# One explicit order of small steps for a chunked recurrence and its MLP on one core

## The chip, the core and the metric

The kernel runs on one core of one Trainium2 chip. The core has five engines that run at the same time and meet through semaphores: TensorE (PE in the profile; its weight loads are PEld), VectorE (DVE), ScalarE (ACT), GpSimd (POOL) and SyncE (SP, which here only issues transfers). Sixteen DMA engines move data between the device memory and the core's SBUF. TensorE writes into PSUM, which the kernel cuts into four tiles of 2 x 512 float32 per partition.

The metric is the time of one execution in microseconds (us) on the device, as a median of runs; less is better.

## The reference

The first half is a recurrence over 768 tokens for 4 batches x 8 heads, with a 40 x 40 state per head:

```python
for t in range(S):
    y[:, :, t] = np.einsum('bhd,bhde->bhe', rt, state)
    Sa = np.einsum('bhde,bhe->bhd', state, at)
    state = state * wt[:, :, None, :] - np.einsum('bhd,bhe->bhde', Sa, bt) \
            + np.einsum('bhd,bhe->bhde', vt, kt)
```

Its output, 3072 rows of 320, goes through an MLP with an exact GELU and 2048 hidden columns:

```python
h = x @ w_in                                    # 320 x 2048
g = 0.5 * h * (1.0 + erf(h / sqrt(2)))
out = g @ w_out                                 # 2048 x 320
```

All inputs of the recurrence are float32. The two weights come out of the set-up as float64, 5.24 MB each; the kernel reads them as pairs of 32-bit words and makes float32 of them on the core.

## The kernel before

**Chunks.** The tokens are cut into 12 chunks of 64 (`C = 64`, `NCH = 12`). In one chunk all 32 heads of all batches are worked on together. The products inside a chunk replace the loop over tokens: the logarithms of w are summed along the chunk (`logs`, `sums`), a, b and k are scaled by the running decays (`scale_a`, `scale_b`, `scale_k`), and four masked 64 x 64 products per head are made: N (b with a), A (k with a), RV (r with v) and M. Since the rank-one term uses the state that it changes, each chunk needs the inverse of a unit triangular 64 x 64 matrix made of N, per head.

**The inverse.** Each 64 x 64 matrix is taken as two triangular 32 x 32 blocks and a corner. `make_N` (L598) makes N in SBUF and stores its diagonal blocks to a scratch tensor in device memory (L615). `start_inverse` (L651) loads them back as `Nb` so that one partition holds one block (L664), and GpSimd builds the inverse `W` column by column: 31 pairs of a product (L672) and a sum (L674). `store_inverse` (L680) writes `W` out again, and `fetch_inverse` (L689) brings it back in the layout of the products, as `Tt` and `T2`. `turn_corner` (L771) transposes it on VectorE into `L`, and `corner` and `joined` (L775, L790) put the corner in with two sets of small matmuls, both into tiles named J. From chunk 2 on the inverse of chunk c+2 is started while chunk c is worked on. The first chunk goes another way: `squares` (L712) inverts its blocks by repeated squaring on TensorE, five stages of 128 small matmuls.

**The chain of a chunk.** With the inverse and the state of the chunk before: `make_X`, `make_sa`, `make_saT`, `make_M`, `make_y2`, `make_QY`, and then `outputs` (L880), which writes the chunk's MLP input `xt`, moves parts of it between partitions by eleven small transfers, and updates the state.

**The MLP.** `mlp(c)` (L986) is a generator: four pieces of the first product, of 40 matmuls each into one PSUM tile, with one GELU each, then the second product. For the first three chunks this is the plain product; from the fourth on `seven` (L937) does it as seven block products instead of eight, with sums of weight blocks made once (`weight_sums`, L929) and sums of activations made by VectorE in each chunk. These pieces fill TensorE's time between the steps of a chunk: `fill()` (L1025) takes the next piece.

**The weights.** `first_load` and `second_load` bring in the words; `to_float` (L312) converts a piece. With VectorE as its engine it is five VectorE operations and one on ScalarE; with GpSimd, three on VectorE, three on ScalarE and two additions on GpSimd (seven of the ten w_in pieces).

**The order.** Each engine works through its own instructions in the order in which the program issues them, and the program issues them by hand: a straight list of calls for the first two chunks (L1060 on) and a loop over the rest (L1247). SP issues almost all transfers, and a transfer that must wait holds up those behind it. Three kinds of calls only keep TensorE busy: `warm` (L1054), `keep` (L92), which makes the next `duo` (L96) begin with such matmuls, and an opening burst of three products.

## Time and profile before

| | |
|---|---|
| time, median of 3 runs | 717.69 us (715.69 to 719.35) |
| span of the profiled execution | 717.1 us (the page gives no other time for it) |
| TensorE busy | 680.9 us (95%) |
| VectorE busy | 365.9 us (51%) |
| GpSimd busy | 348.0 us (49%) |
| ScalarE busy | 222.2 us (31%) |
| first product of the MLP on TensorE (L994) | 220.0 us busy, 1920 instructions |
| second product, seven blocks (L947) / plain (L1011) | 146.4 us / 56.3 us busy |
| moved by DMA | 74.46 MB, mean 104 GB/s |

A float32 matmul call appears in the trace as two instructions, so 40 calls show as x80 and a half piece of the first product (10 calls) as x20. In rows of the timeline the first number is the start in us from the start of the span, the second the length in us; a line number is that of the call or of a helper (all small matmuls have L110), so that the tile names tell them apart. "[12.77 <-DMA Nb<-N]" says that the engine had been idle for 12.77 us until that transfer landed.

### The profile page before, as it was taken

What the parts mean: (1) busy time and instruction counts of PE and PEld (TensorE: products, weight loads), DVE (VectorE), ACT (ScalarE), POOL (GpSimd) and SP (SyncE); (2) the same over time, 40 slices, a digit from 0 to 9 for tenths busy, and PEclk for the clock granted to TensorE, in tenths of its full rate; (3) what the DMA queues carried; (4) which work ended last, traced back from release to release, by engine and by line L of the source; (5) the groups of instructions that cost most, each with busy time, mean ns of one, the idle gap of its engine ahead of it and who ended that gap; (6) DMA issues with size and microseconds to landing.
All of it is one profiled execution on the core that took longest, in us unless ns stands there. A gap on an engine that the chain in (4) does not pass through costs nothing.

```text
span 717.1 us, 32807 instructions
## 1 busy us (share of the span) xinstructions
PE 680.9 (95%) x14816; PEld 584.5 (82%) x14816; DVE 365.9 (51%) x481; ACT 222.2 (31%) x308; POOL 348.0 (49%) x798
## 2 busy tenths in 40 slices
PE   7898897869999999999999999999999999999997
PEld 5565586757777877899899898998998898998987
DVE  2223689995255266276374583573672772522303
ACT  5123575444141240350351332232223413112020
POOL 4374258820760861861862843835826817800000
PEclk8799999989999999999999999999999999999999
DMA  9599437953665755655747646657748553020100
GB/s 132 102 173 151 97 84 185 157 113 87 129 125 96 127 118 94 133 105 94 146 96 128 132 90 125 125 97 127 144 70 155 115 101 66 21 54 3 28 11 18
DMA packets 287923, 74.46 MB, mean 104 GB/s; under 512 B 265736, under 2 KB 284456, under 8 KB 287784
## 3 DMA queue, kind: packets, MB, share of 16 engines
q1 hardware_dynamic: 283360, 68.20, 51.4%
q0 software_dynamic: 864, 2.36, 2.1%
q8 instruction: 116, 1.90, 1.2%
q10 hardware_dynamic: 3560, 1.80, 1.0%
q14 instruction: 23, 0.19, 0.1%
HBM read 58.69 MB, written 9.70 MB: 95 GB/s over the span
## 4 chain that ended last, share of the span: by engine, by line
PE 77%; DVE 3%; SPq 2%; ACT 2%; issue 1%; DMA 1%; ACTq 1%; DVEq 0%
PE ph L994 29%; PE po L947 19%; PE po L1011 7%; PE QY L110 6%; PE J L110 2%; PE X L110 2%; PE av L110 1%; PE sap L110 1%; PE saT_ps L110 1%; PE A_ps L110 1%; PE RV_ps L110 1%; PE M_ps L110 1%; PE N_ps L110 1%; SPq L898 1%; PE wT_ps L110 1%
## 5 line engine op out<-in xcount | busy, mean ns | idle before, releaser
L994 PE MATMUL ph<-xt,w_in_sb 64*128 64x256 f32 x1920 | 220.0, 381 | 0.4 <-issue 0.4
L994 PEld LDWEIGHTS ph<-xt,w_in_sb 64*128 64x128 f32 x1920 | 183.3, 187 | 22.8 <-issue 1.7
L672 POOL TENSOR_TENSOR tmp<-W,Nb 128x126 f32<-128x126 f32 (+22 forms) x310 | 121.3, 391 | 159.4 <-DMA Nb<-N 136.4
L674 POOL TENSOR_TENSOR W<-W,tmp 128x126 f32<-128x126 f32 (+22 forms) x310 | 133.2, 430 | 24.3
L996 ACT ACTIVATE gt<-ph 128x1024 f32<-128x1024 f32 x48 | 49.1, 1023 | 152.3 <-PE ph L994 152.2
L947 PE MATMUL po<-w_out_sb,gt 128*128 128x160 f32 x576 | 82.9, 302 | 1.0 <-DVE gt L967 1.0
L947 PEld LDWEIGHTS po<-w_out_sb,gt 128*128 128x128 f32 x576 | 78.7, 190 | 3.1 <-DVE gt L967 1.3
L1011 PE MATMUL po<-w_out_sb,gt 128*128 128x320 f32 x192 | 56.3, 451 | 2.2 <-ACT wpT L443 2.2
L1011 PEld LDWEIGHTS po<-w_out_sb,gt 128*128 128x128 f32 x192 | 37.0, 197 | 18.1 <-ACT wpT L443 2.5
L803 DVE COPY Tt<-J 32x512 f32<-32x512 f32 x9 | 6.2, 689 | 55.8 <-ACT Tt L803 55.8
L787 ACT COPY Js<-J 128x256 f32<-128x256 f32 x11 | 4.1, 370 | 94.2 <-PE J L110 94.2
L186 DVE STREAM_TRANSPOSE aT<-a_pairs 128x1024 f32<-128x1024 f32 x9 | 11.2, 1246 | 42.3 <-DMA a_pairs<-in_a_dram 42.3
L999 DVE TENSOR_TENSOR half<-gt 128x1024 f32<-128x1024 f32 x9 | 11.4, 1269 | 30.5 <-ACT gt L996 30.4
L951 DVE TENSOR_TENSOR os<-os,po 128x160 f32<-128x160 f32 x36 | 11.5, 319 | 28.9 <-PE po L947 23.2
L947 PE MATMUL po<-extra,half 128*128 128x160 f32 x176 | 26.1, 303 | 0.0
L575 DVE TENSOR_TENSOR SM<-M_ps,upper 128x1024 f32<-128x1024 f32 x12 | 14.5, 1207 | 22.3 <-PE M_ps L110 22.3
L320 ACT ACTIVATE conv<-conv,rebias 128x320 uint32<-128x320 uint32 (+1 forms) x26 | 16.1, 623 | 29.7 <-DVE conv L319 23.3
L947 PEld LDWEIGHTS po<-extra,half 128*128 128x128 f32 x176 | 24.2, 190 | 0.3
L996 ACT ACT_TABLE_LOAD x10 | 12.8, 1283 | 37.1 <-PE ph L994 37.1
L110 PE MATMUL warm<-cum_m,ident 128*128 128x512 f32 x40 | 23.8, 736 | 0.0
L662 POOL MEMSET W<- 128x512 f32 x10 | 5.3, 529 | 35.8 <-DMA inv<-W 35.8
L947 PE MATMUL po<-extra,gt 128*128 128x160 f32 x144 | 21.0, 299 | 0.0
(224 smaller groups left out, 1133.2 us busy)
## 6 DMA issues: line engine op xcount, KB each, us to landing
Nb<-N SPq DMA_DIRECT2D x20, 256.0 KB
VR<-in_v_dram SPq DMA_DIRECT2D x24, 160.0 KB
out_dram<-os SPq DMA_DIRECT2D x48, 80.0 KB
b_rows<-in_b_dram SPq DMA_DIRECT2D x22, 160.0 KB
k_rows<-in_k_dram SPq DMA_DIRECT2D x22, 160.0 KB
N<-N SPq DMA_DIRECT2D x44, 64.0 KB
Tt<-inv SPq DMA_DIRECT2D x44, 64.0 KB
a_pairs<-in_a_dram SPq DMA_DIRECT2D x18, 144.0 KB
```

The costliest lines, as they stand in the source:

```text
L110: nc.tensor.matmul(o, lhsT, rhs, start=first, stop=True, skip_group_check=True)
L186: nc.vector.transpose(to.rearrange("p n (s y) -> p n y s", y=2), raws.pop((c, n)).rearrange("p n (y d) -> p n y d", y=2)[:, :, :, :BL])
L320: nc.scalar.activation(power, power, ACT.Relu, bias=rebias, scale=8.0)
L575: nc.vector.tensor_tensor(to, pt, upper.unsqueeze(1).to_broadcast([P, 2 * G * NP, C]), ALU.mult)
L672: eng.tensor_tensor(t, W[:, :rows, j:j + 1].to_broadcast([P, rows, rest]), Nb[:, j:j + 1, j + 1:].to_broadcast([P, rows, rest]), ALU.mult)
L674: eng.tensor_tensor(W[:, :rows, j + 1:], W[:, :rows, j + 1:], t, ALU.add)
L947: nc.tensor.matmul(po[:, n, :DM // 2], l_[:, f], r_[:, f], start=f == 0, stop=f == NF // 2 - 1)
L951: nc.vector.tensor_tensor(to, one_, other, ALU.add)
L994: nc.tensor.matmul(ph[:, x, s], w_in_sb[half(x), kt, p * P:(p + 1) * P], xt[half(x), kt], start=kt == 0, stop=kt == NK - 1)
L996: nc.scalar.activation(gt[:, 4 * q:4 * q + 4].rearrange("p (x s) t -> p x s t", x=2), ph, ACT.Gelu)
L999: nc.vector.tensor_tensor(s1, block(1, 0), block(1, 1), ALU.add)
L1011: nc.tensor.matmul(po[:, g], gt[:, f, g * P:(g + 1) * P], w_out_sb[:, f], start=f == 0, stop=f == NF - 1)
```

## The change

The hand-written list, the loop and the fill calls go. Every piece of work becomes a generator under a short name, `N`, `inv`, `ph` and so on, whose `yield`s cut it into steps; a string `ORDER` of tokens, one per step, is the order in which all steps of all chunks are issued. A token `ph0:2` is the next step of `ph` for chunk 0, and the number after the colon is the PSUM tile (or conversion buffer) that it takes: four fixed PSUM tiles take the place of a pool that gave them out in turn. Tiles of SBUF are laid out once.

Beside the order itself: no token calls `warm`, and nothing like `keep` is left; the opening burst has six products. The squarings of the first chunk work on two halves of the blocks (`sq0`, `sq1`), with the additions of the identity on VectorE. All weight pieces are converted without GpSimd. A step of the first product is half a piece; one GELU still covers two steps. The second product of the last chunk is the plain one, after a step (`ws4`) that restores a weight block. N of chunk c+1 is made in chunk c, after `corner` of chunk c. Inverses are stored from SP for chunks 1 and 2 and from GpSimd for the others, as before. The decays that scale b and k overwrite the tile of w.

```diff
+POOLED_IN, POOLED_OUT = (), ()
+SCALED_BY_POOL = (0,)
+COPIED_BY_ACT = (1, 2)
+INVERSES_BY_POOL = 3
...
+ORDER = """
+tails0 begin6 w0 begin6:0 consts0 logs0 sums0:1 sums0:2 w1 logs1 sums0 sums0 b0 sums1:3 sc0 sums1:0 a0 zeros4 sums1 b1
+sc1 sums1 gaps0 ta0:2 ta0 pads0 pads3 tb0:1 a1 tails1 ta1:0 gaps1 tb0 N0:3 ta1 r0 tr0:2 tr0 v0 wi0 wi1 k0 N0 sq0 pads1
+tb1:1 sq1 r1 sq1 sq0 sq0:0 sq1:3 zeros0 tb1 sq1 N1:2 sq0 sq0 zeros3 sq1 zeros1 tv0:1 N1 N1 sq1:3 tv0 k1 sq1 sq1 sq1
+sq0:0 r2 sq0 sq0 sq0 RV0:1 ci3:0 b2 ci3 nb1 RV0 pads2 sq0:2 sq0 sq1:3 sq1 sq0 sq0 sq1 inv1 sk0 tk0:0 sq0:1 ci0:1 sq1
...
+ta2 wo0 tn1:0 v2 ci2 tv1 tb2:1 tb2 ci6:1 tk2:2 X1:3 wo2 ci7:2 tk2 tn1 N2:1 N2 N2 ci5:0 ph0:2 ph0 ci6 ci7 ci7 X1 ci5
+ci5 ph0 ph0:0 ph0 wo1 corner1:2 ci8:0 corner1:1 corner1 ci8 A2:3 zeros7 joined1:2 ci6 joined1 joined1 wo4 ph0 A2 RV1:1
...
+co14 co15 co12 co12 ph1 inv2 inv2 ft2 k4 r4 ph1:1 ph1 co13:1 co13 corner2:2 corner2:2 co13 po0 po0 po0 po0 inv3
...
+ph5 ph5 ph5 ph5:1 ph5 ph5 ph5:2 ph5 inv6 inv6 inv6 inv6 tk7:1 ft6 r8 corner6:2 corner6:3 ph5 corner6 v7 RV6:0 RV6
+joined6:1 a8 joined6 joined6 X6:2 inv7 X6 sk7 N7:3 po4 N7 A7:0 A7 saT6:1 saT6 sa6:2 po5:0 sa6 yy6:3:0 M6:1 M6 po5:2
+po5 N7 nb7 tv7 RV7:1 RV7 vp8 QY6 QY6 po5:1 po5 po5 po5:2 po5 po5 w8 y6 logs8 state6 po5 y6 po5 po5:1 po5 tn7:0 po5 ta8
...
+    duos = [psum.tile([P, 2, 512], FP32, tag=f"duo{i}", name=f"duo{i}") for i in range(4)]
...
+    @step
+    def ph(c):
+
+        for q in range(NF // 4):
+            pt = duo().rearrange("p x (s t) -> p x s t", s=2)
+            for s in range(2):
...
+                yield
+            nc.scalar.activation(gt[:, 4 * q:4 * q + 4].rearrange("p (x s) t -> p x s t", x=2), pt, ACT.Gelu)
+            yield
...
+    @step
+    def po(c):
+
+        if c < NS or c == NCH - 1:
+            pt = duo()[:, :, :DM]
+            for piece in range(NF // 4):
+                for g in range(G):
+                    for f in range(4 * piece, 4 * (piece + 1)):
+                        nc.tensor.matmul(pt[:, g], gt[:, f, g * P:(g + 1) * P], w_out_sb[:, f],
+                                         start=f == 0, stop=f == NF - 1)
+                    yield
...
+    for token in ORDER.split():
+        name, *at = token.split(":")
+        places[:] = [int(x) for x in at]
+        if name not in going:
+            kind = name.rstrip("0123456789")
+            going[name] = steps[kind](int(name[len(kind):]))
+        next(going[name], None)
```

The tokens that the text speaks of: `w`, `a`, `b`, `k`, `v`, `r` are loads of a chunk's inputs, `vp`, `bp`, `kp` second loads of v, b and k in another layout; `wi`, `wl`, `wo` are loads of weight words, `ci` and `co` their conversions (w_in in ten pieces, w_out in sixteen); `ta`, `tb`, `tk`, `tv`, `tr`, `tn` are transposes (tn of the state), `sc` and `sk` the scalings of b and k. A chunk's inverse is `N` (product, mask, store), `nb` (the fetch into `Nb`), `inv` (GpSimd's columns and the store), `ft` (the fetch into `Tt` and `T2`), `corner` (`L`, then J) and `joined`. `y` writes `xt` and issues its eleven transfers, `state` updates the state, `ph` is the first and `po` the second product of the MLP.

## The prediction

> **What bounds the kernel now.** I read the page first (shares, slices), then the windows on both sides of one instant, then the timeline around the inverses, then the chain of waits. In the fences "J" is the first product that needs the inverse of a chunk (tile J from L and N), the point where a chunk's chain starts.
>
> ```profile
> span 717.1 us, 32807 instructions
> ...
> PE 680.9 (95%) x14816; PEld 584.5 (82%) x14816; DVE 365.9 (51%) x481; ACT 222.2 (31%) x308; POOL 348.0 (49%) x798
> ...
> PE   7898897869999999999999999999999999999997
> ...
> PEclk8799999989999999999999999999999999999999
> ```
>
> TensorE is 95% busy; holes lie in the first nine slices (18 us each). The windows split the span where the third chunk's J starts (157.1). The first two rows are of all instructions; their first pair is the length and PE's busy time. The third is the same stretch for the tile `warm` alone.
>
> ```profile
> 0.00:157.00 157.00, 130.04 (x3144) 97.40 (x3144) 94.28 (x142) 72.57 (x98) 87.91 (x190) 0.92 0.72 132
> 157.00:717.00 560.00, 550.82 (x11672) 487.12 (x11672) 271.59 (x339) 149.58 (x210) 260.11 (x608) 0.99 0.51 96
> ...
> 0.00:157.00 157.00, 29.32 (x46) 10.08 (x46) 0.92 0.72 132
> ```
>
> After 157 PE idles 9.2 us of 560: nothing but less work can shorten that part. Before 157 it is busy 130.0, of which 29.3 is `warm` and 3.7 more the same filler under other tiles (1.1, 1.0, 0.6, 0.5, 0.5 in the groups by form): about 97 us of needed work in 157. So the gain, if any, is PE work brought forward into the first 157 us.
>
> What sets 157.1 is the inverse of chunk 2, a relay over SP, POOL, SP, DVE:
>
> ```profile
> 116.88 0.24 POOL L672 TENSOR_TENSOR tmp<-W,Nb 128x31 f32<-128x31 f32 x1
> ...
> 148.49 0.23 POOL L674 TENSOR_TENSOR W<-W,tmp 128x16 f32<-128x16 f32 x1
> 149.43 1.28 SPq L686 DMA_DIRECT2D inv<-W  x2
> 153.71 1.93 SPq L696 DMA_DIRECT2D Tt<-inv  x4
> ...
> 156.22 0.71 DVE L773 STREAM_TRANSPOSE L<-Tt 128x512 f32<-128x512 f32 x1
> 157.08 0.89 PE L110 MATMUL J<-L,N 32*32 32x32 f32 x64 [3.37 <-DVE L L773]
> ```
>
> The same relay for a later chunk, to be kept for the change:
>
> ```profile
> 528.70 1.11 PE L110 MATMUL N_ps<-aT,nT 40*64 40x64 f32 x64
> ...
> 532.59 2.02 SPq L615 DMA_DIRECT2D N<-N  x4
> 536.23 1.14 SPq L664 DMA_DIRECT2D Nb<-N  x2
> 542.19 0.24 POOL L672 TENSOR_TENSOR tmp<-W,Nb 128x31 f32<-128x31 f32 x1 [12.77 <-DMA Nb<-N]
> ...
> 574.52 1.64 POOL L686 DMA_DIRECT2D inv<-W  x2 [0.30 <-POOL W L674]
> 579.12 0.85 SPq L696 DMA_DIRECT2D Tt<-inv  x2
> ...
> 582.84 0.71 DVE L773 STREAM_TRANSPOSE L<-Tt 128x512 f32<-128x512 f32 x1 [0.75 <-DMA Tt<-inv]
> ```
>
> N's product to L takes 54.1 us here. PE does not wait, because N is made two chunks ahead.
>
> **The change, part by part.** The sum is made against the profiled execution, span 717.1, 0.6 under the median 717.69; its page gives no other time.
>
> *Work.* The matmuls stay, but for three things. All filler goes (33.0 us); the opening burst grows from 3 to 6 products (six instructions took 0.85 us each, later ones of that shape 0.43: about 7.7 us from 1.6 to 9.3, so chunk 0's first product starts near 9.3 and not 7.4; covered by the wait for transfers below). The last second product takes eight blocks: 4.50 + 4.50 + 8.81 = 17.8 us by chunk 3's rows against 15.4 for the seven at the end: +2.0 to 2.4; I take **+2.0**. Restoring the weight quarter is one 1.5 us DVE operation beside the last first product. Half pieces of the first product issue the same 40 matmuls and one GELU per 1024 columns: nothing.
>
> *Conversions.* Seven of the ten w_in pieces lose two POOL additions (1.4 us each) and gain two DVE operations (0.69): 9.7 us more DVE. Beside POOL's additions the DVE steps were stretched (L321 0.42 to 1.04 us, L319 0.42 to 0.75, L324 0.69 to 0.96 on four pieces: 4.9 us), which goes: net +5. The new order gives DVE about 57 us of work between J of chunk 1 and J of chunk 2, against some 70 us of time: hidden, at nothing. If that cover is gone, each further us of DVE there is a us. The Trainium skill, SBUF — State Buffer, Who interferes with whom, says that a DVE instruction with two SBUF inputs waits out a GpSimd one that reads SBUF, and the reverse. By that rule the out-weight steps beside the inverse stay stretched (3.0 us a piece at 128.4 to 131.3 against 2.4 without), some 10 us more for sixteen; the sum would still be hidden.
>
> *First inverse in halves.* Five squarings ran from 30.7 to 60.4 with filler between; interleaved halves need DVE 15.7 and PE 16.7 us of work, but K of chunk 0 now follows two w_in loads, so I put its end at about 45 and chunk 0's state near 62 (before: 86.9). That is not what is late next: the inverse of chunk 1 is. SP now has, ahead of its fetch of N, eight input loads (327 KB each), wi0 and wi1 (2.1 MB), five more inputs and the store of N. At the windows' 127 to 138 GB/s for inputs (20 us, then 12 us) and 173 GB/s at 0.80 DMA share for w_in (10.5 us), plus 7 for N's way out and in, the fetch lands at 50 (before: 36.9). POOL's 31 columns took 27.5 (36.9 to 64.4) or 28.2 (180.6 to 208.8): 78. Store to fetch 4.6, fetch to L 2.5, L to J 0.9: **J of chunk 1 at 87**, as before (87.6), but with eight attention steps and five pieces of the first product already done.
>
> *Chunk 2's inverse.* SP comes to its fetch only after 15 loads behind chunk 1's fetch (8 w_out pairs at 1.3, inputs at 1.6 to 5.4, N 2.0): 31 us after 83, so 114; landing 4.9, POOL 31.8 (116.9 to 148.7), store 5, fetch and L 3.4: **J of chunk 2 at 159**, 1.9 later than now. PE alone would allow 148: from J to J the order has 60 us of PE work.
>
> *What is done by then.* Counted in the order up to that J: 8 of 8 half pieces of ph for chunk 0 and 8 of 8 for chunk 1, 6 of 8 po pieces, two transposes of chunk 3. Before, by 157: 160 ph matmuls (chunk 0's) and 16 of 64 po matmuls. More: 8 x 2.26 + 4 x 2.2 + 2 x 0.87 = **28.6 us** of PE.
>
> *One chunk of look-ahead less.* N of chunk c+1 is now made just after J of chunk c. PE work between N and its J, by the rows' spacing (ph 2.26, po 2.27, QY 1.5, small products 0.6 to 1.1): 47.8, 49.9, 49.0, 48.2, 48.2, 48.4, 47.2, 48.2, 47.0 us for chunks 3 to 11. The relay in the trace: N to its store 2.65; store to fetch 3.5 to 4.7; fetch to POOL 4.8 to 6.2; POOL 28.2 to 31.4 (less 1.54 for the k scaling, which leaves this place); store to Tt's fetch 4.4 to 6.3; to L 2.5 to 3.7; to J 0.8 and starts 0.3. Median 50.0, fastest 47.1, slowest about 55. PE waits for what is missing: at the medians 15.7 us over nine chunks, at the fastest 0, at the slowest 61. In the new order SP has N's store and fetch side by side in eight of nine chunks, but r, v and a loads stand ahead of N in chunks 6 to 8 and v4, r5 ahead of nb4. I take 49.3 as nearest to the median row: **10 us**.
>
> *End.* The chunk's x rows all go by SP (8.6 us at 468.0, before partly by ACT); 11.3 us of second product cover them. One more us for two copies and four stores: +1.0; waits at 167 (1.1) and 672 (1.0) go.
>
> Sum: 717.1 + 1.9 - 28.6 + 2.0 + 10 + 1.0 - 2.1 = **701.3 us**, forecast 701.
>
> **Rivals.**
> *The relay becomes the bound (slower).* Without waits the sum is 691.3, so 25.8 us of waits undo it: a relay of (433.9 + 25.8) / 9 = 51.1 us on average decides. For it: L waited for Tt in two of the last chunks even with two chunks of room, and 54.1 above. Against it: nothing else stands between the steps in the new order. At 53 us: 43 of waits, **734**. Chance 0.20.
> *No wait at all.* Relay at 47 to 48, J of chunk 2 by PE near 150: 717.1 - 7 - 28.6 + 2.0 - 1.1 = **682**. The fastest rows all have to meet. Chance 0.15.
> *The start is late by DVE.* All 26 conversions at stretched lengths (+16 us) use up the cover; J of chunk 2 at 171: **713**. DVE was at 98% from 100 to 150 before. Chance 0.08.
> *The clock.* Filler gone, PE waits in the first 90 us. Where the trace has no filler and waits of 2 to 3 us (150 to 170), the granted clock fell to 0.87 and 0.79, and 64 sums took 1.99 against 1.16 us at 0.71. If the 57 us before the first J all ran so: 98 us, J at 105, +18: **719**. I give it little, since transfers and POOL, not PE, set that J. Chance 0.07. The Trainium skill, TensorE: Matmul & The Clock Gate, Why this matters for your kernels, asks for no PE gap over about 3 us; by that rule the pads were worth keeping, and the trace agrees so far that the clock fell at such gaps.
>
> **How the numbers follow.** The forecast has 0.50, its own range 690 to 713 (relay 48 to 50.5, J of chunk 2 at 154 to 164). 0.5% of 717.7 is 3.6 us, about what a measurement tells here: faster is under 714, slower over 721. Faster: 0.15 + most of 0.50 + a little of the DVE rival = 0.67; same 0.10 (upper edge of the forecast, DVE and clock rivals); slower 0.23. The range 682 to 724 leaves out half of the no-wait case's low side and most of the relay rival.
>
> **What will show it.** J of chunk 1 near 87 and of chunk 2 near 159, no `warm` but the opening, 16 ph half pieces before 157; from then a chunk every 51 to 52 us with a wait of PE for L of about 1 us in each; last store 5 us after the last matmul. Wrong if J follows J by 54 us or more, or if J of chunk 2 comes after 170.

## The result and the profile after

The kernel after takes 799.11 us (median of 4, 796.02 to 805.32), the kernel before 716.69 us (median of 4, 713.29 to 719.35): a ratio of 1.1145, interval 1.1069 to 1.122. The prediction was 701, with 682 to 724 as its range. It is wrong by its sign, and its line "wrong if J follows J by 54 us or more" came true.

The page of the profile after, its span and busy rows, two rows of slices, the queue that brings the instructions, and the chain that ended last:

```profile
span 795.2 us, 32559 instructions
...
PE 700.3 (88%) x14724; PEld 622.0 (78%) x14724; DVE 368.2 (46%) x504; ACT 212.2 (27%) x295; POOL 339.8 (43%) x781
...
PE   8768998967898997997898998889798899898997
...
PEclk9888989978997997898899798899998899899999
...
q8 instruction: 115, 1.88, 1.0%
...
PE 45%; SPq 17%; POOL 12%; DMA 10%; issue 10%; DVE 3%; ACT 1%; DVEq 0%; ACTq 0%; POOLq 0%
```

TensorE (PE) has 19.4 us more busy time although the 33.0 us of filler are gone, and it idles 94.9 us where it idled 36.2. The holes are no longer in the first slices alone; they come back all along the span, and so does a lowered clock (the mean granted clock is 0.911, before 0.979). The chain that ended last runs over SP's queue, POOL and the transfers for 39% of the span. "issue" (time in which an engine waited for nothing that the profile shows) is 10%, where before it had 1%.

The windows on both sides of J of chunk 2, again in the columns length, PE busy, PE weight loads, DVE, ACT, POOL, granted clock, DMA share, GB/s:

```profile
0.00:168.60 168.60, 140.24 (x3308) 117.55 (x3309) 110.60 (x197) 68.55 (x93) 72.16 (x173) 0.91 0.69 136
168.60:795.20 626.60, 560.06 (x11416) 504.40 (x11416) 257.63 (x308) 143.61 (x202) 267.67 (x608) 0.91 0.43 82
```

These two rows hold the whole account against the sum of 701.3. J of chunk 2 comes at 168.6 and not at 159: +9.6. After it the sum had 550.8 - 28.6 + 2.0 = 524.2 us of PE work and 18.1 of idle time; measured are 560.1 busy, +35.9, and 66.5 idle, +48.4. Together 93.9, which is 795.2 - 701.3. The busy part is put down to the clock, 0.91 where the same kind of work had 0.99; the run with long fill below bears the size out. The idle part is in the waits of PE (us in total, times, longest, over the whole run):

```profile
PE duo L140 <- issue: 51.8, 41, 3.5
PE duo L140 <- DVE conv L826: 19.5, 6, 5.6
```

Of the first, 36.4 us fall after J of chunk 2 (37.5 with 1.1 us of the same kind under another line); of the second, 13.9 us, since its longest wait is the one right at that J:

```profile
168.62 1.08 PE L140 MATMUL duo<-conv,N 32*32 32x32 f32 x64 [5.57 <-DVE conv L826]
```

In the kernel before, the wait for the inverse (L, which in the kernel after is `conv` of L826) and the largest of its issue waits were these:

```profile
PE J L110 <- DVE L L773: 4.1, 2, 3.4
...
PE saT_ps L110 <- issue: 2.1, 2, 1.8
```

**The issue stalls.** The timeline of PE after J of chunk 5; rows of the products between two inverses, with a stall in brackets:

```profile
374.62 1.11 PE L140 MATMUL duo<-Tt,avs 64*64 64x64 f32 x61
...
376.81 0.27 PE L140 MATMUL duo<-Tt,avs 64*64 64x64 f32 x2 [1.08 <-issue]
...
380.28 0.27 PE L140 MATMUL duo<-aT,kT 40*64 40x64 f32 x2 [1.33 <-issue]
...
384.29 0.47 PE L140 MATMUL duo<-rT,late 40*64 40x64 f32 x3 [1.92 <-issue]
384.69 7.40 PE L1030 MATMUL duo<-w_out_sb,gt 128*128 128x160 f32 x32
...
747.94 4.51 PE L1030 MATMUL duo<-w_out_sb,gt 128*128 128x160 f32 x32
```

A stall falls into the middle of one product, where nothing that it reads can be late, and again after 3.5 and 4.0 us. The queue q8 explains the place. Its 115 packets of 16,384 bytes stand against 14,724 matmul and 14,724 weight-load records: 29,448 = 115 x 256 and a rest of 8. Stalls that follow each other begin on the same place of this count, 256 instructions apart (over the whole run the place creeps from the 181st to the 48th, so some entries of the queue must have no record here), 1.2 to 1.8 us after one of those packets ended; a packet takes 1.1 us on average. From a packet's start to the first instruction out of it are 2.2 to 3.0 us. A product of 32 calls is 128 instructions and takes 1.05 us, so 256 of them run out in some 2.2 us and PE waits for the rest of the fetch. One half piece of the first product is 40 instructions in 2.26 us: there the fetch is hidden. Before, long pieces stood between the small products and the 116 fetches cost some 5 us.

The last two rows show what follows a stall: the same 32 matmul records take 7.40 us here and 4.51 later. The windows of the stretch around the third stall, 3.4 us each:

```profile
380.20:383.60 3.40, 2.09 (x128) 1.95 (x128) 1.23 (x1) 0.00 (x0) 0.00 (x0) 1.00 0.48 75
383.60:387.00 3.40, 2.71 (x12) 2.60 (x13) 2.14 (x2) 0.00 (x0) 0.00 (x0) 0.50 0.35 93
387.00:390.40 3.40, 3.40 (x14) 3.40 (x14) 1.34 (x2) 0.00 (x0) 0.68 (x3) 0.50 0.96 185
390.40:393.80 3.40, 3.40 (x92) 3.23 (x95) 0.33 (x1) 1.65 (x3) 2.69 (x10) 1.00 0.88 170
```

A stretch in which PE was busy for 2.09 of 3.40 us is followed by one at half clock, which lasts until a stretch without such holes has gone by. If the clock is always either full or half, as in these rows, then with a mean of 0.911 over 795.2 us, (1 - 0.911) x 2 x 795.2 = 142 us ran at half speed; before, (1 - 0.979) x 2 x 717.1 = 30 us. After J of chunk 2 the clock fell 14 times: eight times behind a stall put down to issue (55 us at half clock), four times behind a wait for L (41 us), twice behind other waits (7 us). The Trainium skill, TensorE: Matmul & The Clock Gate, Why this matters for your kernels, names idle gaps over about 3 us as what brings the clock down; here gaps of 1.1 to 1.9 us did. The Trainium skill, TensorE: Matmul & The Clock Gate, A second HAM failure mode: psum-queue depth-cycling, tells of frequent short idles that do it, and that is the reading which this trace agrees with.

**The relay.** The inverse of chunk 5 in rows of PE, SP, POOL and DVE, from the J before it (306.56) over N (307.32) to its own J (368.28):

```profile
306.56 0.83 PE L140 MATMUL duo<-conv,N 32*32 32x32 f32 x64 [3.26 <-DVE conv L826]
307.32 1.16 PE L140 MATMUL duo<-aT,nT 40*64 40x64 f32 x64
...
312.13 3.09 SPq L658 DMA_DIRECT2D N<-spare  x4
317.15 1.20 SPq L711 DMA_DIRECT2D Nb<-N  x2
...
322.29 0.24 POOL L726 TENSOR_TENSOR tmp<-W,Nb 128x31 f32<-128x31 f32 x1 [18.18 <-DMA Nb<-N]
...
354.31 1.64 POOL L735 DMA_DIRECT2D inv<-W  x2 [0.30 <-POOL W L728]
...
361.76 2.43 SPq L745 DMA_DIRECT2D Tt<-inv  x4
...
367.52 0.70 DVE L826 STREAM_TRANSPOSE conv<-Tt 128x512 f32<-128x512 f32 x1
...
368.28 1.08 PE L140 MATMUL duo<-conv,spare 32*32 32x32 f32 x64 [3.95 <-DVE conv L826]
```

N to J takes 61.0 us here. Means over chunks 3 to 11, read from the same rows of every chunk, beside the terms of the prediction:

| step | in the prediction | before, measured | after, measured |
|---|---|---|---|
| N to its store | 2.65 | 3.0 | 4.9 |
| store to fetch of Nb | 3.5 to 4.7 | 3.9 | 5.3 |
| fetch to POOL's first column | 4.8 to 6.2 | 5.4 | 4.8 |
| POOL | 28.2 to 31.4, less 1.54 | 31.3 | 30.8 |
| POOL's end to the fetch of Tt | 4.4 to 6.3 | 6.3 | 5.9 |
| to L | 2.5 to 3.7 | 4.1 | 3.9 |
| L to J | 0.8 + 0.3 | (waits for PE) | 1.5 |
| N to J | 49.3 taken | 53.5, with 1.1 for the last step and less 1.54 | 57.1 |

From J to the next N are 3.3 us (0.7 to 5.7). J follows J by (723.6 - 239.8) / 8 = 60.5 us. That N to J and J to N add up to this period is so in any order; what shows that the loop binds is that PE stood waiting for L at J of chunks 4, 5, 6, 7 and 9. At the other four J, L lay ready first and PE was late.

The wait for L is 19.5 us of the idle time of the whole run; the stalls are more than twice that.

### The profile page after: what moved, and what is told of

The parts are those of the page before. It is cut to its first block, busy times and chain, and to the rows that moved or that the text cites. A ratio compares the mean times of both kernels' runs of the same rounds, so it can differ in the third digit from the quotient of the medians.

```text
span 795.2 us, 32559 instructions
## 1 busy us (share of the span) xinstructions
PE 700.3 (88%) x14724; PEld 622.0 (78%) x14724; DVE 368.2 (46%) x504; ACT 212.2 (27%) x295; POOL 339.8 (43%) x781
## 4 chain that ended last, share of the span: by engine, by line
PE 45%; SPq 17%; POOL 12%; DMA 10%; issue 10%; DVE 3%; ACT 1%; DVEq 0%; ACTq 0%; POOLq 0%
PE duo L140 19%; PE duo L992 12%; PE duo L1030 8%; POOL W L728 6%; POOL tmp L726 6%; SPq L215 5%; PE duo L1014 4%; SPq L218 2%; SPq L204 2%; PE duo L504 2%; DMA inv<-W 2%; SPq L950 2%; DMA w_tile<-in_w_dram 2%; DMA Nb<-N 2%; DMA r_pairs<-in_k_dram 1%
## 5 line engine op out<-in xcount | busy, mean ns | idle before, releaser
L992 PE MATMUL duo<-xt,w_in_sb 64*128 64x256 f32 x1920 | 213.1, 379 | 1.2 <-DMA xt<-xt 0.8
L992 PEld LDWEIGHTS duo<-xt,w_in_sb 64*128 64x128 f32 x1920 | 188.8, 188 | 24.6 <-issue 4.2
L995 ACT ACTIVATE gt<-duo 128x1024 f32<-128x1024 f32 x48 | 49.2, 1024 | 121.6 <-PE duo L992 121.6
L1030 PE MATMUL duo<-w_out_sb,gt 128*128 128x160 f32 x512 | 80.6, 319 | 1.1 <-issue 1.1
L1030 PEld LDWEIGHTS duo<-w_out_sb,gt 128*128 128x128 f32 x512 | 77.4, 206 | 2.2 <-issue 1.3
L1014 PE MATMUL duo<-w_out_sb,gt 128*128 128x320 f32 x256 | 77.0, 460 | 0.0
L1014 PEld LDWEIGHTS duo<-w_out_sb,gt 128*128 128x128 f32 x256 | 51.0, 203 | 22.7 <-issue 4.6
L140 PE MATMUL duo<-rT,late 40*64 40x64 f32 x1536 | 37.5, 249 | 13.9 <-issue 13.9
L140 PEld LDWEIGHTS duo<-rT,late 40*64 40x64 f32 x1536 | 33.1, 161 | 16.7 <-issue 16.4
L1030 PE MATMUL duo<-extra,conv 128*128 128x160 f32 x256 | 36.8, 302 | 0.0
L1030 PEld LDWEIGHTS duo<-extra,conv 128*128 128x128 f32 x256 | 35.0, 190 | 0.9
L623 DVE TENSOR_TENSOR SM<-duo,upper 128x1024 f32<-128x1024 f32 x12 | 14.6, 1219 | 28.6 <-PE duo L140 28.6
```

Source lines behind the costliest of these rows:

```text
L140: nc.tensor.matmul(o, lhsT, rhs, start=first, stop=True, skip_group_check=True)
L992: nc.tensor.matmul(pt[:, x, s], w_in_sb[half(x), kt, p * P:(p + 1) * P], xt[half(x), kt], start=kt == 0, stop=kt == NK - 1)
L995: nc.scalar.activation(gt[:, 4 * q:4 * q + 4].rearrange("p (x s) t -> p x s t", x=2), pt, ACT.Gelu)
L1014: nc.tensor.matmul(pt[:, g], gt[:, f, g * P:(g + 1) * P], w_out_sb[:, f], start=f == 0, stop=f == NF - 1)
L1030: nc.tensor.matmul(pt[:, n, :DM // 2], l_[:, f], r_[:, f], start=f == 0, stop=f == NF // 2 - 1)
```

## The experiments

Theory A, after these readings: the dense runs of small products are the loss (stalls, then half clock), and the wait for L is what they bring with them. Theory B: the relay's loop is the loss, and PE's stalls fall into time in which it would wait anyway. Theory C: the lowered clock is the loss, and anything that keeps PE busy, long or short, holds it up. Theory D came out of the first runs: both limits lie close together, the loop at 60.5 us a chunk and PE's own pace a little below it, so that either cut alone shows little. In the diffs the places of PSUM after the colon are left out, and the tokens of one chunk stand for all.

**N before J (look).** N, its store and its fetch ahead of the J before, the dense products left together:

```diff
-tb6 tk6 ft5 corner5 corner5 ... joined5 tn5 ta6 N6 RV5 joined5 joined5 saT5 po4 saT5 w7 RV5 N6 N6 sa5 nb6 sa5 A6 A6
+N6 nb6 ft5 corner5 corner5 ... joined5 tn5 RV5 joined5 joined5 saT5 po4 saT5 w7 RV5 sa5 sa5 A6 A6
```

> Edit: from chunk 4 on, the product N, its store and its fetch Nb are moved before the J of the chunk before (N into the first product's pieces), so a chunk's inverse has a chunk more of room; the small products stay back to back. Theory A (PE runs dry of instructions where small products stand back to back: the changed kernel has 41 idle stretches put down to issue, 51.8 us, and the clock falls behind them): only PE's waits for L go (19.5 us to under 6), the issue idles stay near 50 us, time 775 to 785. Theory B (the relay N - store - fetch - POOL - store - fetch - L is the bound, the rival of the prediction): the period falls from 60 us to the 50 us of PE work, nine chunks, time 715 to 735, and the issue idles go with it.

853.2 us, ratio 1.1913 (1.1846 to 1.198). Neither expectation held.

```profile
PE duo L140 <- issue: 47.2, 38, 2.9
PE duo L140 <- DVE aT L535: 29.2, 6, 7.7
PE duo L140 <- DVE conv L826: 25.1, 4, 11.5
```

An N that stands earlier needs its own inputs earlier, and those loads had kept their places in SP's queue: aT is late now. The relay's fetch of Tt came 19 to 37 us after POOL's end in six of nine chunks: the edit puts N6 and nb6 ahead of ft5, so on SP the fetch of a finished inverse stands behind the store and the fetch of the next N, which was late. N to J grew to 77.9 us. So this edit does not give the inverse the room that was meant, and is no test of theory B.

**Pieces between the small products (inter), and both edits (both).**

```diff
-ft5 corner5 corner5 ... joined5 joined5 saT5 po4 saT5 w7 RV5 N6 N6 sa5 nb6 sa5 A6 A6 yy5 M5 ... M5 po4 po4 po4 QY5 QY5
+ft5 a7 corner5 corner5 N6 po4 corner5 RV5 N6 po4 RV5 N6 nb6 ... joined5 X5 po4 joined5 joined5 X5 po4 po4 po4 A6 saT5 sa5
+A6 po4 saT5 sa5 yy5 M5 po4 M5 logs7 po4 po4 po4 QY5 QY5
```

The run with both edits has that, and N ahead of J as well:

```diff
+ph5 ph5 ph5 N7 ph5 N7 ph5 N7 ph5 inv6 nb7 inv6 ft6 sc7 a8 ph5 corner6
```

> Edit: from chunk 3 on, the second product's pieces are put between the small products, one after every two or three of them; N still follows the J of the chunk before, as in the changed kernel. Theory A (instructions): issue idle of PE from 52.9 us to under 20, time at half clock from 140 us to 60 to 90, time 725 to 750. Theory B (relay): the idles put down to issue turn into waits for L (19.5 us to some 60), time 785 to 805. Theory C (the clock falls by itself once the filler is gone, whatever the order): issue idle falls, half clock stays near 140 us, time 755 to 770.

853.2 us, ratio 1.1884 (1.1814 to 1.1955).

> Edit: both at once from chunk 3 on: N, its store and fetch a chunk earlier, and pieces of the first and the second product between the small products. Theory A (instructions, with the relay as the second cause): issue idle under 15 us, waits for L under 6 us, half clock under 70 us, time 695 to 715, under the kernel before. Theory B (relay alone): as the run with the earlier N alone, 715 to 735. Theory C (clock falls without filler): 730 to 750.

921.9 us, ratio 1.2868 (1.2821 to 1.2915). The waits of PE in the first of the two:

```profile
PE duo L1030 <- DVE os L1034: 36.5, 6, 8.1
PE duo L140 <- issue: 33.5, 25, 3.1
PE duo L504 <- DVE st L964: 26.9, 8, 3.5
```

The stalls fell (51.8 to 33.5, and 24.6 with both edits), but the second product's blocks now follow so close on each other that PE waits for VectorE to take the block before out of PSUM (`os`), and the state is late. With both edits the turn that N needs (nT) was late by 66.2 us in all. Orders that I wrote by hand traded one wait for another; that the stalls were the loss could be read from none of the three. In the run with both edits nb7 stands ahead of ft6 too, and the fetch of Tt came 39 us after POOL's end on average.

**Long matmuls into the dense runs (filler).** Work is added that nothing uses: 56 pairs of 128 x 512 products, two calls each, five or six to a chunk.

```diff
+    @step
+    def fill(c):
+        pt = duo()
+        for n in range(2):
+            mm(pt[:, n], ident, cum_m.unsqueeze(1).to_broadcast([P, 4, P]))
...
-tn5 corner5 joined5 tn5 ta6 N6 RV5 joined5 joined5 saT5 po4
+tn5 fill17 corner5 joined5 tn5 ta6 N6 fill18 RV5 joined5 joined5 saT5 fill19 po4
```

> Edit: the changed kernel with 56 pairs of matmuls of 128x512 added that nothing reads (0.43 us each at the full clock, 48 us in all), one pair after every two small products that stand back to back, from chunk 1 to 10. Theory A (instructions): while a pair runs, instructions arrive, so the issue idles fall from 52.9 us to under 20 and the clock holds: time 755 to 785, faster than the changed kernel although PE has 48 us more to do. Theory B (relay): N comes later after J by the fillers between them, time 800 to 820. If neither idle nor clock changes: 799 + 48 = 847.

814.6 us, ratio 1.1356 (1.1293 to 1.1419). The fill came out at 113.8 us of PE in 224 records, not 48; the forecast of the time missed by that. 113.8 us of added work cost 15.5 us.

```profile
PE duo L144 <- issue: 20.0, 16, 4.0
PE duo L144 <- DVE conv L830: 4.3, 3, 2.0
```

The stalls went to 20.0, the wait for L to 4.3, the clock to 0.969. PE was busy 766.5 us; less the fill that leaves 652.7, and the kernel's own products taken alone cover 661.6 (the two overlap at their edges), against 700.3 in the kernel after: some 39 to 48 us of those 700.3 are slowed work. J followed J by 62.1 us. PE waited for L at only three J, 4.3 us in all, and was busy for 95% of the span, so PE with its fill set the pace and hardly the loop. The fill ran in the time that stalls, slow clock and waits for L had taken. The time lies in theory B's range, but the waits that B gave as the reason are not there; the mechanism is theory A's.

**The same fill in small products (shortfill).** 60 calls of 64 x 64 x 64 in each of the 56 places, and one small copy by ScalarE:

```diff
-        for n in range(2):
-            mm(pt[:, n], ident, cum_m.unsqueeze(1).to_broadcast([P, 4, P]))
+        for n in range(15):
+            for e in range(2):
+                for j in range(2):
+                    mm(pt[half(e), j, n % 8 * C:(n % 8 + 1) * C], ident[half(j), half(j)], cum_m[half(j), half(j)])
+        nc.scalar.copy(junk, pt[:, :, 0])
```

> Edit: the run with 56 long fillers again (it took 814.6 us: TensorE at 113.8 us of filler, yet only 15 us more time), but each filler is 60 calls of 64x64x64, about the same 2 us of TensorE work in 240 instructions in place of 8, and a copy of two columns by ACT that ends it. Theory A (instructions): such a filler needs nearly a whole fetch of 256 instructions itself, so it gives no time to catch up: issue idles of PE 50 us or more, time 870 to 930. Theory C (what helps is only that PE is kept busy, for the clock): 805 to 825, like the long one.

954.0 us, ratio 1.3283 (1.3225 to 1.334).

```profile
PE duo L144 <- issue: 110.7, 86, 3.4
```

13,440 more PE instructions are 52.5 blocks of 256, and the instruction queue brought 53 more packets (168). 45 more stalls of 1.3 us are 58.9 us of waits. The two fills stand in the same places and differ mainly in the number of their instructions; one takes stalls away, the other doubles them. That is what shows that the stalls come from instructions running out. Theory C falls with it, since a fill of about the same 2 us that kept PE busy made the kernel 155 us slower.

**The kernel before, made dense (b_dense).** Four fill calls of each chunk from 3 on are made after `make_QY`, and not between the small products:

```diff
+        owed = []
+        between = fill if c == 2 else lambda: owed.append(1)
...
-            fill()
+            between()
...
+        fill(len(owed))
```

> Edit: the kernel before, with the four fill() calls that stand between corner and make_QY moved behind make_QY in chunks 3 to 11; the inverse keeps its two chunks of room. So only the new order's habit of setting a chunk's small products back to back is copied. Theory A (PE runs dry of instructions in such stretches, and the clock falls behind the stalls): issue idles of PE go from 5 to 30 to 50 us, half clock from 31 us to over 90 us, time 760 to 800. Theory B (the relay is the bound): nothing of it is touched, 715 to 725.

853.5 us, ratio 1.1891 (1.1836 to 1.1946): right in its direction, and too low.

```profile
PE QY L110 <- DVE SM L575: 62.7, 10, 9.7
```

The larger part is another cost of a dense order: nothing stands between a small product and VectorE's answer to it (the mask of M, 1.2 us of work, here waited for by up to 9.7). In the rows at 319 us VectorE has the mask standing behind a turn of a later chunk's a, and that turn waits 7.96 us for its load; so part of this cost belongs to the place where the turn stands in this edit. Stalls (26 us over all tiles) and a clock of 0.879 come beside it.

**The kernel before with one chunk of look-ahead (b_ahead).** N of the next chunk is made at the start of the chunk before, and its inverse fetched at that chunk's end:

```diff
+        if c > 2 and more:
+            make_N(n)
+            steps = start_inverse(n, nc.gpsimd)
...
-            make_N(n2)
-            steps = start_inverse(n2, nc.gpsimd)
...
+        if more:
+            fetch_inverse(n)
+            turn_corner(n)
```

> Edit: the kernel before, with N of chunk c+1, its store, its fetch and the start of its inverse moved behind the corner of chunk c (chunks 4 to 11), and the fetch of the inverse to the end of the chunk; the pieces of the MLP stay between the small products. So only the lost chunk of look-ahead is copied. Theory A (instructions first): PE waits for L by some us a chunk, no issue idles, time 725 to 745. Theory B (the relay is the bound): the period goes to about 60 us as in the changed kernel, 780 to 805.

814.6 us, ratio 1.1348 (1.1305 to 1.139).

```profile
PE J L110 <- DVE L L773: 67.0, 11, 8.2
```

N to J is 60.4 us over the chunks that the edit reaches (4 to 11) and J to N 1.0, and J follows J by 61.4, with a wait for L of 5.2 to 8.2 us at each: a loop of this length alone, made so by one chunk less of look-ahead and without the dense order and with almost no stalls (under 10 us), costs the kernel before more than the whole change did. The clock fell here too, to 0.907, so waits for L bring it down as stalls do. The size is not that of the loop in the kernel after: the fetch of Tt came 10 to 13 us after POOL's end, where there it came at 5.9. The edit puts it at the end of the chunk, on SP behind the loads and the store of the MLP's output (before J of chunk 5, SP comes to that store at 357.20 and to the fetch at 361.8).

**The loop cut (stale).** In the kernel after, J takes the inverse of the chunk before, so the fetch doesn't wait for POOL:

```diff
-        iv = stored.pop(c)
+        iv = stored[c - 1 if c > 2 else c]
```

> Edit: the changed kernel, where from chunk 3 on the fetch Tt takes the inverse of the chunk before (it lies ready), so that no product waits for this chunk's inverse; all work is still done, and the result is that of another inverse. Theory A (instructions): only the waits for L go (19.5 us) and a little of the half clock, issue idles stay at 45 to 55 us: 765 to 785. Theory B (relay): 700 to 740.

783.4 us, ratio 1.0893 (1.084 to 1.0946), as theory A had it; 16 us less than the kernel after.

```profile
PE duo L140 <- issue: 57.3, 46, 3.2
PE duo L140 <- DVE conv L826: 15.2, 4, 5.0
```

J follows J by 58.8 us, with 57.3 us of stalls: PE's own limit in this order is that or a little less. What is left of the waits for L is SP's order: the fetch stands behind loads (from 346.9 to 357.1 before the one for J of chunk 5).

**A third attempt to part the two (mix, mix_stale).** The half pieces of the first product between the small products, once with the loop, once with the cut of the run before:

```diff
-tn5 corner5 joined5 tn5 ta6 N6 RV5 joined5 joined5 saT5 po4 saT5 w7 RV5 N6 N6 sa5 nb6 sa5 A6 A6 yy5 M5 ... QY5 QY5
+tn5 ph4 corner5 joined5 tn5 ta6 N6 ph4 ph4 RV5 ph4 joined5 joined5 saT5 ph4 ph4 saT5 w7 RV5 N6 N6 sa5 nb6 sa5 A6 ph4 A6
+yy5 ph4 ph4 M5 ph4 ... QY5 QY5 ph4 ph4
```

> The same steps as the changed kernel in every chunk from 2 on, but the half pieces of the MLP's first product are put between the small products that follow J (one or two at a time) instead of standing together, and a part of the second product follows late. N still follows J, but later, since pieces stand between. Nothing is left out. Theory D (two limits: the loop of J, N and the inverse's relay; and TensorE's work with its instruction stalls): the stalls fall, to under 20 us, and the loop grows by what now stands between J and N and between the steps of the relay on POOL and SP, so that J follows J by 65 to 72 us and the time is 820 to 870 us, with waits of PE for L. Rival R (the stalls and the lowered clock are the whole loss, the relay's wait only fills time that they leave): with the stalls gone the time falls to 720 to 745 us.

> The order of the run that has the half pieces between the small products, and J takes the inverse of the chunk before (from chunk 3 on; the output is then another than the reference's), so that the loop over the relay is cut and everything else stays: the same products, transfers and relay steps. Theory D: with neither long dense stretches nor the loop, what is left is TensorE's own work of about 50 us a chunk, with stalls and lowered clock of 2 to 4 us: 168 + 9 x 53 + 70 gives 715 to 750 us, J following J by 52 to 56 us. Rival L (the instruction stalls are harmless, only the loop counts): the same as the changed kernel with that cut alone, 775 to 790 us. Rival R: the same as the run with the loop kept, within 10 us.

911.5 us (1.2702, 1.2644 to 1.2761) and 911.8 us (1.2739, 1.2657 to 1.2821). The stalls fell as said, to 18.8 and 21.7 us, and the loop grew beyond what D gave. But the cut changed nothing, so the pair can't do what it was made for. The reason stands in SP's rows (and POOL's store of the inverse, whose landing POOL's next row waits for at 366.72) before J of chunk 5 in the run with the loop:

```profile
368.09 4.12 SPq L215 DMA_DIRECT2D v_pairs<-in_v_dram  x8
372.60 3.96 SPq L1004 DMA_DIRECT2D out_dram<-os  x4
...
381.08 2.01 SPq L745 DMA_DIRECT2D Tt<-inv  x4
...
360.87 1.63 POOL L735 DMA_DIRECT2D inv<-W  x2 [0.30 <-POOL W L728]
366.72 0.53 POOL L719 MEMSET W<- 128x512 f32 x1 [4.22 <-DMA inv<-W]
```

The inverse had landed by 366.7, its fetch went at 381.1. Ahead of it on SP stands the store of the MLP's output, which waits for the second product's last blocks, and these now came later, and behind it two more loads. Rival R fell (no 720 to 745), L and D are left undecided by these two: the coupling is SP's queue, which the cut leaves whole.

**Filler of the kernel before away (b_nofill).** `warm` and `keep` return at once:

```diff
-        asked[:] = [columns]
+        return
...
-        pt = duo("warm")
+        return
```

> Edit: the kernel before without its filler (warm and keep issue nothing; the opening burst stays), so TensorE has about 29 us less to do, nearly all of it before 157 us. Theory C (the filler is what keeps the clock up): half clock from 31 us to over 60 us in the first 160 us, time 725 to 745. Otherwise: the first 157 us are set by transfers, POOL and DVE, so time 712 to 722.

719.62 us against 719.98, ratio 0.9989 (0.9965 to 1.0012). The first 160 us of this run:

```profile
0.00:160.00 160.00, 120.72 (x3094) 102.36 (x3094) 93.98 (x141) 72.89 (x98) 88.05 (x190) 0.80 0.69 128
```

The clock there fell to 0.80 (0.92 with the filler, for 0 to 157) and PE's busy time by 9.5 us over the run and not by 33.0, so 23 us came back as slowed work; and neither moved the median. (The run with the profile took 723.1 us, the slowest of its ten; J of chunk 2 came at 162.0 in it.) J of chunk 2 waited for L, 3.9 us here and 3.4 with the filler: the relay of transfers and POOL set it, with or without. Theory C falls for the start as well.

**Chunk 2's fetch earlier (nb2_early).** The fetch of N of chunk 2 right behind its store on SP:

```diff
-tk2 tn1 N2 N2 N2 ci5 ph0
+tk2 tn1 N2 N2 N2 nb2 ci5 ph0
...
-state1 RV2 nb2 co7
+state1 RV2 co7
```

> Edit: the changed kernel with one token moved: the fetch of N of chunk 2 (nb2) from behind the weight loads, where SP came to it at 120.7 us, to directly behind the store of N at 100.6. Theory E (the start: SP's queue makes the inverse of chunk 2 late): the fetch goes out at 104 to 106, POOL begins near 112 instead of 127.8, J of chunk 2 at 152 to 156 instead of 168.6, and as the chunks behind it follow at their own period, time 783 to 790. If conversions on DVE or PE's own work set that J: 165 to 169, time 795 to 800.

801.6 us, ratio 1.121 (1.1156 to 1.1264). POOL's first column, in this run:

```profile
112.22 0.24 POOL L726 TENSOR_TENSOR tmp<-W,Nb 128x31 f32<-128x31 f32 x1 [24.34 <-DMA Nb<-N]
```

It began at 112.2 where it had begun at 127.8, and J of chunk 2 came at 170.9 where it had come at 168.6. Where the 15.6 us went stands further on in this run:

```profile
143.15 0.23 POOL L728 TENSOR_TENSOR W<-W,tmp 128x16 f32<-128x16 f32 x1
...
158.82 1.29 SPq L735 DMA_DIRECT2D inv<-W  x2
...
166.84 0.70 DVE L826 STREAM_TRANSPOSE conv<-Tt 128x512 f32<-128x512 f32 x1
...
170.92 0.75 PE L140 MATMUL duo<-conv,N 32*32 32x32 f32 x64
```

The finished inverse lay for 15.4 us until SP came to its store, behind loads, mostly of output weights, that SP issued only between 148.7 and 157.6. L came 0.9 us earlier than in the kernel after (166.84 against 167.76), so the run does not make the relay early, and theory E as it was meant is not decided. What the two runs do show: in the kernel after, J of chunk 2 waited 5.57 us for L, PE's own products having ended at 163.1, so SP's queue did make it late, by that much; an earlier L alone could have won these 5.6 us and not the 13 to 17 that theory E gives. In this run J did not wait; PE came to it 3.4 us after L.

**The same steps in other orders (order3, order4, order5, order6).** All tokens in another order, with the loop and the instruction blocks weighed against each other. The chunk shown before, in order4:

```diff
+N6 po3 po3 X5 sk6 ph4 nb6 ph4 v6 tk6 po3 ph4 corner5 corner5 r7 A6 A6 corner5 ph4 joined5 joined5 po3 joined5 ph4 sa5 ph4
+ph4 saT5 sa5 ph4 ta7 saT5 ph4 yy5 M5 po4 po4 M5 w7 tv6 QY5 QY5 po4 tr7 av6 bp7 vp7 po4 y5 po4 state5 po4 ...
+... inv6 inv6 sums7 sums7 ta7 tb7 a8 ft6 N7 N7 sums7 ph5 N7 X6 po4 inv7 tn6 X6 ph5 tn6 RV6 nb7 ph5 RV6 ph5 ph5 corner6
```

N of chunk 6 now stands ahead of `corner` of chunk 5, its loads and turns earlier still, and a piece of the MLP in nearly every gap.

> Edit: the changed kernel with its ORDER rearranged throughout (the same steps, tiles and instructions; only the order of the tokens and the PSUM tiles they take differ). It was arranged against the durations of the traces so far with both limits in mind: N is made before the J of the chunk before, so that from N to J there are some 60 us or more, and seldom more than one small product stands between two pieces of the MLP. Theory D (two limits that lie close together, the loop J - N - relay - J at 60.5 us and TensorE's own work with its instruction stalls and lowered clock at 57 to 58 us a chunk, so that removing one shows little): with both gone the period falls to 51 to 54 us, issue idle under 20 us, waits for L under 12 us, granted clock over 0.96, time 690 to 720. Theory C (the clock falls without filler): granted clock stays near 0.91 whatever the waits, 730 to 760.

742.65 us, ratio 1.0324 (1.0293 to 1.0355): 56 us under the kernel after, and above what I gave. Stalls 14 us, the wait for L 17.5 us, clock 0.961.

> The same steps as the changed kernel in another order throughout; nothing is left out. The order was searched by the two limits: a full instruction fetch for every 256 TensorE instructions that is not hidden by long matmuls, and the relay's loop with SP's and POOL's queues, each with its durations from the traces here. N comes earlier, so that the relay has room, and pieces of the MLP stand between the small products. Theory D (only both limits together bring the time back): waits of PE for L under 8 us in all and issue stalls under 12 us, the granted clock 0.97 or more, J following J by 50 to 53 us, and 695 to 725 us. The rival (the new steps themselves cost more, by their halves, copies and conversions, whatever the order): 735 to 760 us, as the earlier rearranged order.

> A second order found in the same way from another start, which leaves more instruction stalls (about twice those of the one before by the same working) and smaller waits elsewhere. Theory D: 698 to 730 us, within 1% of the one before. The rival: 735 to 760 us.

723.46 us (1.0059, 1.0031 to 1.0087) and 730.42 us (1.0146, 1.0122 to 1.017). Windows and waits of order4:

```profile
0.00:156.00 156.00, 129.73 (x3242) 106.32 (x3244) 98.58 (x176) 65.26 (x88) 66.84 (x170) 0.87 0.74 144
156.00:719.90 563.90, 548.56 (x11484) 471.30 (x11480) 272.14 (x329) 150.36 (x210) 280.19 (x611) 1.00 0.50 92
```

```profile
PE duo L140 <- issue: 5.3, 6, 1.9
PE duo L140 <- DVE conv L826: 4.2, 2, 3.6
```

J follows J by 51.8 us. With the same steps, transfers and conversions the order alone (with the PSUM tiles that it gives to each step) gives back 76 of the 82 us. It changes the loop, the instruction blocks and SP's queue at once, so it does not part their shares. The rival of these two runs (the new steps themselves cost more) falls. order5 has 20 us of stalls and is 7 us behind.

> The fourth order with five of the six products of the opening burst moved into two waits of TensorE for loads at 25 to 29 us (three of them) and 38 to 42 us (two); the number of instructions is the same, so that the instruction fetches fall where they fell. Theory K (the lowered clock in the first 156 us, where it was 0.87, costs TensorE time that the later order can use): the clock rises to 0.91 or more there, J of chunk 2 comes 3 to 8 us earlier than 173.7, and the time is 712 to 721 us. Rival (loads and the relay set the start): the same as the fourth order within 3 us, 720 to 727.

720.46 us against 716.86, ratio 1.0052 (1.0029 to 1.0075): the same as order4. The clock hardly rose (0.88 in the first 156 us, where order4 has 0.87; J of chunk 2 at 174.7), so that theory K got no fair test. No order of the new steps that I tried beats the kernel before. What the last 4 us are stays open: in the profiled runs order4 needs 563.9 us from 156 on and the kernel before 561.1, too small a difference to be read from one profile of each.

## Why the prediction was wrong

*Where the gain was looked for.* "PE work brought forward into the first 157 us" is what the change does: by J of chunk 2 all 16 half pieces of ph and 6 of 8 pieces of po were done, and the 28.6 us are right as a count. But this gain was at most 28.6 us, and the terms after it lost 84.

*One chunk of look-ahead less* is the step that failed. It was the right place, and its price was wrong twice over.
1. The relay was put at 49.3 us and took 57.1. The means over nine chunks of the kernel before, which its trace had ready, give 53.5, above the 51.1 that the prediction itself names as deciding; I had taken ends from a few chunks and put the value near their median. The rest, 3.6 us, lies mostly in N's store (+1.9), the fetch of Nb behind it (+1.4) and POOL (+1.1 after the 1.54 that were taken off). By the prediction's own rule this size alone turns the sign: 9 x 57.1 - 433.9 = 80 us of waits where it had 10. PE's measured waits for L after J of chunk 2 are 13.9 us, since PE's own time had grown into that room, which is the second point.
2. "PE waits for what is missing" took for granted that PE's work needs the time that its rows add up to. In the dense order it needs more: the sum had no term for instructions that run out. The rows before show it: the fetch of 256 instructions is there too, hidden by long pieces. This term is 37.5 us after J of chunk 2. With it come 35.9 us of slowed work, from a clock that fell behind these stalls and behind the waits for L alike.

These two don't add up one by one: the loop at about 60 us and PE's own pace of at most 58.8 (the run with the loop cut) lie side by side, so that taking the loop away gives 16 us, and adding 113.8 us of fill costs 15.5. How many of the 82 us each of the two would cost alone in this order stays open.

*First inverse in halves.* The fetch landed at 49.5 (predicted 50). POOL's 31 columns took 36.3 us and not 27.5, beside VectorE's conversions: their busy time rose from 22.8 to 29.8 us, with rows of 0.59 to 0.86 us near the end where the same shapes had taken 0.25 to 0.4. Taken with the steps behind POOL, L was ready near 93.8 and J of chunk 1 came at 95.0, not 87. The prediction stretched VectorE's conversions by such overlap and forgot POOL's side. The Trainium skill, SBUF — State Buffer, Who interferes with whom, has it both ways (a VectorE instruction with two SBUF inputs blocks a GpSimd one that reads SBUF, and the reverse); the trace agrees, with 36.3 against 27.5; of the 20 rows that took at least 1.4 times as long as before, 19 lie beside a VectorE instruction that combines two tensors, nearly always one of a conversion. Chunk 0's state was there at 73 and not 62.

*Chunk 2's inverse.* The relay set this J, as the prediction has it, with larger terms: SP came to the fetch at 120.7 (predicted 114), POOL began at 127.8 and took 33.7 us (31.8), and J came at 168.6 after a wait for L of 5.57 us (predicted 159, wrong from 170). "PE alone would allow 148" was 15 us too early: PE's own products ended at 163.1, since from J of chunk 1 PE began 8 us late and was busy for 63.7 us and not 60, with small waits besides.

*Work.* The last second product took 17.49 us (predicted 17.8), the end came 5.2 us after the last store was issued. The removed filler was counted as 33.0 us gone from PE's work, and put to use in the first 157 us; the run without filler shows it worth nothing to the time (0.9989), as the rival "the clock" half said.

*The rivals.* "The relay becomes the bound" is what happened, at 0.20, with 734 as its price: right in kind, too low, since its relay was 53 and not 57.1, and it too had no stalls and no slow clock. "The clock" was looked for in the start alone, where it did little; it cost some 36 us after J of chunk 2, behind stalls and waits, where the prediction took PE to be as full as before. "No wait at all" did not come. The rival of the late start had its 171 nearly right, but PE waited there for L, by a late fetch on SP.

*The range* reached to 724 and left out 799, since no case joined two of these: a relay that is too long for its room, and dense small products that run out of instructions, with a clock that falls behind both.

## What to carry to other kernels

Ask of an order not only what each engine has to do, but where the loops close: sum a relay over DMA and several engines with its mean over all its rounds, and set it against the work that stands beside it. Where small matmuls stand together, count instructions as well as microseconds: here 256 PE instructions had to last about 2.5 us, and a long piece between small products pays for itself by hiding both the fetch and the other engines' answers. An in-order queue that serves both the relay and the rest (SP here) couples the two: in six runs here (look, inter, both, b_dense, b_ahead, mix) the fetch of an inverse came on average 13 to 39 us after POOL's end, against 5.9 in the kernel after, with the output's store, loads or the next N ahead of it on SP.

## What the runs showed of the hardware

TensorE's instructions came in packets of 16,384 bytes, one for every 256 instructions (115 and 29,448 after, 168 with 13,440 more). A packet took 0.9 to 1.55 us; where 256 small instructions ran in 2.2 us, PE stood still for 1.1 to 1.9 us, in the middle of a product, once every block.

The clock fell to one half after a stretch of 3.4 us in which PE was busy for 2.09 us, with no single gap over 1.92 us, and it stayed down in steps of that length. In the kernel after, PE was busy for at most 2.49 us in the 3.4 us before each of the 20 falls; but some stretches with less (the least 1.60 us) brought none, so these runs give no threshold. About 142 us of the kernel after ran at half clock, 50 us with the long fill, about 43 us in order4.

In the start of the kernel before, the clock was worth nothing: at 0.80 for 160 us the time was 719.6, with the filler that kept it up 720.0.
